# Weights converted a few operations per half step from the end of the attention on, and a 64-float tile of biases: a two-layer feed-forward kernel behind an attention

## The chip, the cores and the metric

The kernel runs on one core of one Trainium2 chip. The time is that of one execution on the device, in microseconds (us). It is given as the median of three runs. Apart from these runs, one execution was profiled, and the rows below come from its trace.

## The reference, cut to what matters

```python
# attention of 8 batches, 8 heads, 576 positions of 64; k and v are averaged over 8 positions first
x = attention(q, k, v)                    # -> 4608 tokens x 512
h = x @ w_in1;  x = (h * cos(h)) @ w_out1           # 512 -> 2048 -> 512
h = x @ w_in2;  return (h * clip(h + 3, 0, 6) / 6) @ w_out2
```

The weights of the two layers arrive as 64-bit numbers.

## The kernel before

**Weights.** The hidden width of 2048 is cut into NF = 16 pieces `fc` of 128. A piece of a layer has two halves, w_in and w_out, and each half is one job. `fetch_weights` (L89) loads the 64-bit words of a job into a tile `st`. `convert_weights` (L101) makes fp32 out of them and splits them into a high and a low part, `wh` and `wl`. A job has three operations in the code, `first`, `second` and `third`; on the engines these are four instructions on DVE (L115, L119, L124, L127), two on ACT (L114, L132) and one on POOL (L133). There are 64 jobs. The pieces 0 to 6 lie in `pool_a`; the pieces 7 to 15 lie in `pool_b`, which is opened when the attention has ended and its memory is free. The second layer's pieces take the same places when the first layer's are used up.

**Steps.** A block is 512 tokens. A step (m, key, bl, fc) is one layer, one block and one piece. `gemm1` (L164) makes h out of the block's x: 12 matmuls of 512 columns, with the weights as the stationary operand (loaded into the array ahead of the matmul) and `xh`, `xl` as the moving one. `chain0` to `chain3` apply the activation on ACT and DVE and split the result into `gh` and `gl`. `gemm2` (L220) follows two steps later, with 12 more matmuls of 512 columns. In the first layer `wh`, `wl` are stationary and `gh`, `gl` moving there; in the second layer it is the other way round. On PE, the 12 matmuls of gemm1 and the 12 of an earlier step's gemm2 alternate.

There are 59 steps for the pieces 0 to 6 (0 to 4 in the first two blocks) of the first layer, with the attention woven in between; then 85 steps for its other pieces, and 144 for the second layer, 16 to a block. Steps are numbered from 0 in that order: step 59 is the first without a piece of attention due, steps 144 to 287 are the second layer.

**When a job is issued.** `need(s)` (L587) is called for step s and for step s+1. It issues every job up to the one asked for, whole. So the code asks for piece 7 when step 60 is issued.

**What sets the order on the engines.** The code's order is only a priority. The tile framework sorts the instructions when the program is built, engine by engine, by a plan of its own in which an instruction may go as soon as its operands and its buffers are there. A job that the code issues late can so be placed much earlier. At run time each engine follows the order that was built.

**Where tiles lie.** Pools lie behind each other in a partition's memory in the order in which they are opened: `pool_a`, `stg`, `xpl` (xr, xh, xl), `gpl` (`bias_c` first, then g, t, gh, gl, ys), then the attention's `ap`, and in its place later `pool_b` and `ypl`.

Of the kernel before, what the change touches and what calls it, by code (L numbers as in the profile page):

```python
# [8 lines left out]
F32 = mybir.dt.float32  # L9
# [15 lines left out]
def f(ap):  # L25
    return ap.bitcast(F32)
# [3 lines left out]
def tile_kernel(ctx, tc, q, k, v, wi1, wo1, wi2, wo2, ident_d, mask_d, out):  # L30
# [3 lines left out]
    P = 128  # L34
# [4 lines left out]
    NF = wo1.shape[0] // P  # L39
# [3 lines left out]
    LAG = 2  # L43
# [32 lines left out]
    pool_a = ctx.enter_context(tc.tile_pool(name="pool_a", bufs=NA))  # L76
    stg = ctx.enter_context(tc.tile_pool(name="stg", bufs=1))
    xpl = ctx.enter_context(tc.tile_pool(name="xpl", bufs=1))
    gpl = ctx.enter_context(tc.tile_pool(name="gpl", bufs=1))
# [9 lines left out]
    def fetch_weights(m, fc, half):  # L89
        st = stg.tile([P, 2 * HW], U32, tag="st", name="st", bufs=2)  # L90
        wi, wo = words[m]
        if half == 0:
            nc.sync.dma_start(
                out=st.rearrange("p (c j) -> p c j", j=2 * P),
                in_=wi[:, fc * 2 * P : (fc + 1) * 2 * P].rearrange("(c p) j -> p c j", p=P),
            )
        else:
            nc.sync.dma_start(out=st, in_=wo[fc * P : (fc + 1) * P, :])
        staged[m, fc, half] = st

    def convert_weights(m, fc, half, pool):  # L101
        st = staged.pop((m, fc, half))
        if half == 0:
            weights[m, fc] = tuple(
                pool.tile([P, 2 * HW], F32R, tag=nm, name=nm) for nm in ("wh", "wl")
            )
        wh, wl = (t[:, half * HW : (half + 1) * HW] for t in weights[m, fc])
        lo, hi = st[:, 0::2], st[:, 1::2]
        a = stg.tile([P, HW], U32, tag="a", name="a", bufs=AB)
        e = stg.tile([P, HW], BF16, tag="e", name="e")  # L110
        w = f(a)

        def first():
            nc.scalar.activation(out=e, in_=st.bitcast(BF16)[:, 3::4], func=AF.Square)  # L114
            nc.vector.tensor_scalar(  # L115
                out=a, in0=hi, scalar1=0x07FFFFFF, scalar2=3,
                op0=ALU.bitwise_and, op1=ALU.logical_shift_left,
            )
            nc.vector.scalar_tensor_tensor(  # L119
                out=a, in0=lo, scalar=29, in1=a, op0=ALU.logical_shift_right, op1=ALU.bitwise_or  # L120
            )

        def second():
            nc.vector.scalar_tensor_tensor(  # L124
                out=a, in0=hi, scalar=0xC0000000, in1=a, op0=ALU.bitwise_and, op1=ALU.bitwise_or
            )
            nc.vector.scalar_tensor_tensor(  # L127
                out=w, in0=e, scalar=2.0**-30, in1=w, op0=ALU.is_ge, op1=ALU.mult
            )

        def third():
            nc.scalar.activation(out=wh, in_=w, func=AF.Copy)  # L132
            nc.gpsimd.tensor_tensor(out=wl, in0=w, in1=f(wh), op=ALU.subtract)  # L133

        return [first, second, third]
# [16 lines left out]
        nc.gpsimd.tensor_tensor(out=xl, in0=t, in1=f(xh), op=ALU.subtract)  # L152
        xs_[key, c] = (xh, xl)

    bias_c = gpl.tile([P, 32], F32, tag="bias", name="bias_c")
    nc.vector.memset(bias_c[:, 0:1], 0.25)
    nc.vector.memset(bias_c[:, 1:2], math.pi / 2)
    nc.vector.memset(bias_c[:, 2:3], 3.0)
# [5 lines left out]
    def gemm1(s):  # L164
        m, key, bl, fc = steps[s][:4]
        wh, wl = weights[m, fc]
        pool = ps_h2 if ps_h2 is not None and s % 2 else ps_h
        h = pool.tile([P, N], F32, tag="h", name="h")
        n = 0
        for c in range(NC):  # L170
            cs = slice(c * P, (c + 1) * P)
            xh, xl = xs_[key, c]
            for a, z in ((wh, xh), (wh, xl), (wl, xh)):
                nc.tensor.matmul(h, a[:, cs], z, start=(n == 0), stop=(n == 3 * NC - 1))  # L174
                n += 1
        hs[s] = h
# [357 lines left out]
    for bl in range(NB):  # L534
        n = NAL[bl]
        steps += [(0, (0, bl), bl, fc, fc == 0, fc == n - 1) for fc in range(n)]
    SA = len(steps)
    for bl in range(NB):
        n = NAL[bl]
        steps += [(0, (1, bl), bl, fc, fc == n, fc == NF - 1) for fc in range(n, NF)]  # L540
    SB = len(steps)
# [22 lines left out]
    live = True  # L564

    wjobs = [(0, fc, hf, "a") for fc in range(NA) for hf in range(2)]
    fetched = 0
    converted = 0

    def w_fetch():  # L570
        nonlocal fetched
        if fetched < len(wjobs) and fetched < converted + 2:
            fetch_weights(*wjobs[fetched][:3])
            fetched += 1

    running = []
    whole = set()

    def w_ops(n):
        while running and n:  # L580
            running.pop(0)()
            n -= 1
            if not running:
                whole.add(wjobs[converted - 1][:3])
                w_fetch()

    def need(s):  # L587
        m, _, _, fc = steps[s][:4]
        while (m, fc, 1) not in whole:
            w_convert(pool_a if wjobs[converted][3] == "a" else pool_b)  # L590

    def w_convert(pool, n=3):
        nonlocal converted
        m, fc, hf, _ = wjobs[converted]
        converted += 1
        running.extend(convert_weights(m, fc, hf, pool))
        w_ops(n)

    w_fetch()
    w_fetch()  # L600
    npieces = 0
    while not started:
        next(att)
        npieces += 1
        while converted < len(WPRE) and WPRE[converted] <= npieces:
            w_convert(pool_a)
    for c in range(NC):
        fetch_x(0, (0, 0), 0, c)
    for c in range(NC):
        split_x((0, 0), c)  # L610

    pool_b = None
    T = len(steps)
    after = {}
    ypl = None
# [1 line left out]
    for slot in range(2 * (T + LAG) + 4):  # L617
        s, odd = divmod(slot, 2)
        for fn in after.pop(slot, ()):
            fn()  # L620
        if not odd and s < T:
            m, key, bl, fc, first, last = steps[s]
            need(s)
            gemm1(s)
            chain0(s)
            chain1(s)
            chain2(s)
            chain3(s)
            if s + LEAD < T and (pool_b is not None or steps[s + LEAD][3] < NA):
                need(s + LEAD)  # L630
            if key[0] == 1 and fc == NF - 5:
                for c in range(NC):
                    t = ypl.tile([P, N], F32, tag="yv", name="yv", bufs=4)
                    nc.sync.dma_start(
                        out=t, in_=yp_d[c * P : (c + 1) * P, bl * N : (bl + 1) * N]
                    )
                    yprev[key, c] = t
            nxt = s
            while nxt < T and steps[nxt][1] == key:
                nxt += 1  # L640
            left = nxt - s
            if nxt < T:
                nm, nk, nbl = steps[nxt][:3]
                ready = nk[0] != 0 or min(B - 1, ((nbl + 1) * N - 1) // S) in done
                if (nk, 0) not in xraw and (nk, 0) not in xs_ and ready and left <= 4:
                    for c in range(NC):
                        fetch_x(nm, nk, nbl, c)
                    for c in range(2):
                        after.setdefault(slot + max(1, 2 * (left - 2) + 1 + c), []).append(
                            lambda nk=nk, c=c: split_x(nk, c)  # L650
                        )
                    after.setdefault(slot + 2 * (left - 1) + 1, []).append(
                        lambda nk=nk: [split_x(nk, c) for c in (2, 3)]
                    )
        if odd and s >= LAG and s - LAG < T:
            gemm2(s - LAG)
        while converted - len(WPRE) < len(WAT) and WAT[converted - len(WPRE)] <= slot:
            w_convert(pool_a)
        if live:
            key = steps[s][1]  # L660
            i = sum(1 for x in steps[:s] if x[1] == key)
            goal = base + 32 * (key[1] + (2 * i + odd + 1 + PACE) / (2 * NAL[key[1]]))
            if key[0] > 0:
                goal = 1 << 30
            elif slot < len(GOFF):
                goal += GOFF[slot]
            while live and npieces < goal:
                try:
                    next(att)
                    npieces += 1  # L670
                except StopIteration:
                    live = False
                    actx.close()
                    ps_h2 = ctx.enter_context(tc.tile_pool(name="ps_h2", bufs=2, space=PSUM))
                    pool_b = ctx.enter_context(tc.tile_pool(name="pool_b", bufs=NF - NA))
                    ypl = ctx.enter_context(tc.tile_pool(name="ypl", bufs=1))
                    wjobs += [(0, fc, hf, "b") for fc in range(NA, NF) for hf in range(2)]
                    wjobs += [(1, fc, hf, "a") for fc in range(NA) for hf in range(2)]
                    wjobs += [(1, fc, hf, "b") for fc in range(NA, NF) for hf in range(2)]
                    w_fetch()  # L680
                    w_fetch()
# [48 lines left out]
```

## Time and profile before

| | us |
|---|---|
| median of three runs (lowest, highest) | 1875.38 (1873.78, 1876.55) |
| the profiled execution | 1878.48 |
| its span, first to last instruction | 1876.6 |
| PE busy | 1790.0 |
| DVE busy | 927.4 |
| ACT busy | 875.2 |
| POOL busy | 403.7 |

The span is the time from the first to the last instruction on the core; the 1.9 us beside it lie before and behind. The profiled execution is 3.1 us above the median of the runs. Busy times are unions over an engine's instructions. The stretches of the second group below begin where gemm1 of steps 0, 41, 63, 142 and 147 begins, and the last ends within gemm1 of step 287.

### The profile page before, as it was taken

Reading aid. Unit: us, or ns where it says so; the run is one execution under the profiler, and the core shown is the slowest. Engines: PE = TensorE matmul, PEld = TensorE weight load, DVE = VectorE, ACT = ScalarE, POOL = GpSimd, SP = SyncE. Lnnn points to the kernel's source line nnn. Section 1 sums busy time; section 2 is a strip of 40 time slices with the busy share of each in tenths; the row PEclk is TensorE's granted clock in tenths of the full one; section 3 lists DMA queues with packets and bytes.
Section 4 is the critical chain, followed back from the end, with each engine's and each line's share of the span. In section 5 each row is a group of like instructions: output and inputs, shape, how many; then the busy total and the mean of one; then the engine's idle time right before and its main releaser. Section 6 shows DMA issues by size and latency. Waiting matters only on the chain.

```text
span 1876.6 us, 21118 instructions
## 1 busy us (share of the span) xinstructions
PE 1790.0 (95%) x8016; PEld 1446.5 (77%) x8016; DVE 927.4 (49%) x1386; ACT 875.2 (47%) x1472; POOL 403.7 (22%) x302
## 2 busy tenths in 40 slices
PE   5689999999888999999999899999999999999999
PEld 4567777888666888888888678888888888888887
DVE  7999656656989364444445952222222222222222
ACT  3567677776666455555555533232323232322222
POOL 3755344322433111111112421010101010100000
PEclk8789999999998999999999999999999999999999
DMA  7656352223434022222222411010101010101000
GB/s 203 180 164 209 113 155 73 88 74 121 154 127 146 23 90 68 68 68 68 68 68 79 129 62 45 1 45 1 45 1 45 1 45 1 45 2 39 1 23 23
DMA packets 114630, 138.82 MB, mean 74 GB/s; under 512 B 44256, under 2 KB 68960, under 8 KB 114528
## 3 DMA queue, kind: packets, MB, share of 16 engines
q1 hardware_dynamic: 114528, 137.47, 23.8%
q8 instruction: 63, 1.03, 0.2%
q14 instruction: 39, 0.32, 0.1%
HBM read 99.69 MB, written 37.75 MB: 73 GB/s over the span
## 4 chain that ended last, share of the span: by engine, by line
PE 77%; DVE 12%; issue 4%; ACT 3%; DMA 2%; POOL 1%; SPq 0%; DVEq 0%; POOLq 0%; ACTq 0%
PE h L174 36%; PE y L236 36%; DVE a L119 2%; PE ap_ps L392 2%; DVE a L124 2%; PE ap_ps L468 2%; DVE a L127 1%; DVE a L115 1%; DVE g L195 1%; DVE raw L321 1%; DVE gl L217 1%; POOL xl L152 1%; DMA raw<-in_k_dram 1%; DMA xr<-x_d 1%; DVE g L208 1%
## 5 line engine op out<-in xcount | busy, mean ns | idle before, releaser
L174 PE MATMUL h<-xl,wh 128*128 128x512 f32 x1152 | 457.5, 397 | 13.4 <-POOL xl L152 13.3
L174 PE MATMUL h<-xh,wh 128*128 128x512 f32 x1152 | 459.1, 399 | 2.3 <-ACT xh L151 2.3
L174 PE MATMUL h<-xh,wl 128*128 128x512 f32 x1152 | 456.6, 396 | 0.0
L152 POOL TENSOR_TENSOR xl<-xr,xh 128x512 fp32r<-128x512 f32 x108 | 151.1, 1418 | 948.3 <-ACT xh L151 947.0
L200 DVE SCALAR_TENSOR_TENSOR g<-g,h 128x512 f32<-128x512 f32 x144 | 98.9, 687 | 471.1 <-ACT g L186 471.1
L186 ACT ACTIVATE g<-h,bias_c 128x512 f32<-128x512 f32 x144 | 98.9, 687 | 437.8 <-PE h L174 437.3
L174 PEld LDWEIGHTS h<-xl,wh 128*128 128x128 f32 x1152 | 217.6, 189 | 67.8 <-POOL xl L152 19.6
L211 ACT ACTIVATE gh<-g 128x512 fp32r<-128x512 f32 x288 | 181.7, 631 | 180.5 <-DVE g L200 104.4
L217 DVE TENSOR_TENSOR gl<-g,gh 128x512 fp32r<-128x512 f32 x255 | 190.6, 747 | 145.5 <-ACT gh L211 143.6
L174 PEld LDWEIGHTS h<-xh,wh 128*128 128x128 f32 x1152 | 217.4, 189 | 50.9 <-ACT xh L151 3.8
L174 PEld LDWEIGHTS h<-xh,wl 128*128 128x128 f32 x1152 | 217.3, 189 | 49.1 <-issue 0.4
L236 PE MATMUL y<-gh,wh 128*128 128x512 f32 x576 | 233.6, 406 | 9.2 <-ACT ys L252 5.3
L236 PE MATMUL y<-gl,wh 128*128 128x512 f32 x576 | 232.1, 403 | 5.3 <-DVE gl L217 5.2
L236 PE MATMUL y<-gh,wl 128*128 128x512 f32 x576 | 230.7, 401 | 0.0
L236 PE MATMUL y<-wh,gh 128*128 128x512 f32 x576 | 226.4, 393 | 1.4 <-DVE yv L244 1.4
L236 PE MATMUL y<-wl,gh 128*128 128x512 f32 x576 | 226.2, 393 | 0.0
L236 PE MATMUL y<-wh,gl 128*128 128x512 f32 x576 | 225.9, 392 | 0.0
L195 DVE SCALAR_TENSOR_TENSOR g<-g,t 128x512 f32<-128x512 f32 x144 | 114.9, 798 | 156.2 <-ACT g L194 156.0
L184 ACT ACTIVATE t<-h 128x512 f32<-128x512 f32 x144 | 85.3, 593 | 117.6 <-PE h L174 117.5
L236 PEld LDWEIGHTS y<-gh,wh 128*128 128x128 f32 x576 | 111.1, 193 | 37.4 <-ACT ys L252 7.8
L198 ACT ACTIVATE g<-g 128x512 f32<-128x512 f32 x144 | 90.9, 631 | 96.0 <-DVE g L195 95.7
L236 PEld LDWEIGHTS y<-gl,wh 128*128 128x128 f32 x576 | 111.0, 193 | 31.9 <-DVE gl L217 8.9
(93 smaller groups left out, 2140.4 us busy)
## 6 DMA issues: line engine op xcount, KB each, us to landing
xr<-x_d SPq DMA_DIRECT2D x72, 256.0 KB, 2.8
st<-in_moe_w_in_dram SPq DMA_DIRECT2D x32, 512.0 KB, 3.8
st<-in_moe_w_out_dram SPq DMA_DIRECT2D x32, 512.0 KB, 3.3
yp_d<-ys SPq DMA_DIRECT2D x36, 256.0 KB, 2.5
yv<-yp_d SPq DMA_DIRECT2D x36, 256.0 KB, 3.5
xr<-y_d SPq DMA_DIRECT2D x36, 256.0 KB, 2.7
out_dram<-ys SPq DMA_DIRECT2D x36, 256.0 KB, 2.0
raw<-in_k_dram SPq DMA_DIRECT2D x8, 1024.0 KB, 5.8
```

The source lines that it names most:

```text
L119: nc.vector.scalar_tensor_tensor(out=a, in0=lo, scalar=29, in1=a, op0=ALU.logical_shift_right, op1=ALU.bitwise_or)
L124: nc.vector.scalar_tensor_tensor(out=a, in0=hi, scalar=0xC0000000, in1=a, op0=ALU.bitwise_and, op1=ALU.bitwise_or)
L152: nc.gpsimd.tensor_tensor(out=xl, in0=t, in1=f(xh), op=ALU.subtract)
L174: nc.tensor.matmul(h, a[:, cs], z, start=(n == 0), stop=(n == 3 * NC - 1))
L184: nc.scalar.activation(out=t, in_=hs[s], func=AF.Copy, bias=0.25, scale=INV_2PI)
L186: nc.scalar.activation(out=g, in_=hs[s], func=AF.Relu, bias=bias_c[:, 2:3], scale=1.0)
L195: nc.vector.scalar_tensor_tensor(out=g, in0=g, scalar=MAGIC, in1=t, op0=ALU.subtract, op1=ALU.subtract)
L198: nc.scalar.activation(out=g, in_=g, func=AF.Sin, scale=-TWO_PI)
L200: nc.vector.scalar_tensor_tensor(out=g, in0=g, scalar=6.0, in1=h, op0=ALU.min, op1=ALU.mult)
L211: nc.scalar.activation(out=gh, in_=g, func=AF.Copy)
L217: eng.tensor_tensor(out=gl, in0=gs[s][0], in1=f(gh), op=ALU.subtract)
L236: nc.tensor.matmul(y[c], a, z, start=(first and n == 0), stop=(last and n == 2))
```

## The change

**The jobs.** `w_ahead` is new. From the end of the attention on it is called in each half step, and it issues one operation of the running job in an even half step and two in an odd one, so one job per step. For the second layer's pieces in `pool_a` it issues an operation in odd half steps alone, a job in three steps, and not before step SA + 2 = 61; a piece fc in `pool_b` is not begun before step SB - 16 + fc + 2. `need` stays as the last resort.

**The tile.** `bias_c` is 256 bytes of a partition instead of 128. Three of its columns are used, before and after.

```diff
-    bias_c = gpl.tile([P, 32], F32, tag="bias", name="bias_c")
+    bias_c = gpl.tile([P, 64], F32, tag="bias", name="bias_c")
...
     def need(s):
         m, _, _, fc = steps[s][:4]
         while (m, fc, 1) not in whole:
-            w_convert(pool_a if wjobs[converted][3] == "a" else pool_b)
+            if running:
+                w_ops(len(running))
+            else:
+                w_convert()
...
+    def w_ahead(s, odd):
+        if not running:
+            if converted == len(wjobs):
+                return
+            m, fc, _, home = wjobs[converted]
+            if m == 1 and s < (SA + LAG if home == "a" else SB - NF + fc + LAG):
+                return
+            w_convert(0)
+        m, _, _, home = wjobs[converted - 1]
+        slow = m == 1 and home == "a"
+        w_ops(odd if slow else 1 + odd)
...
+        if not live:
+            w_ahead(s, odd)
```

**What it does to the order.** PE has the same instructions in the same order, all 7858. The other engines have the same instructions too, and their order differs at one place alone, within four steps that follow soon after the attention. On DVE, where L115 to L127 are a job's instructions and L195, L208, L217 those of the chain, there stands in the kernel before:

```order
L119 SCALAR_TENSOR_TENSOR a<-st,a 128x512
L195 SCALAR_TENSOR_TENSOR g<-g,t 128x512
L127 SCALAR_TENSOR_TENSOR a<-e,a 128x512
L124 SCALAR_TENSOR_TENSOR a<-st,a 128x512
L208 TENSOR_TENSOR g<-h,g 128x512
L127 SCALAR_TENSOR_TENSOR a<-e,a 128x512
L217 TENSOR_TENSOR gl<-g,gh 128x512
L115 TENSOR_SCALAR a<-st 128x512
```

and at the same place in the changed kernel:

```order
L127 SCALAR_TENSOR_TENSOR a<-e,a 128x512
L195 SCALAR_TENSOR_TENSOR g<-g,t 128x512
L119 SCALAR_TENSOR_TENSOR a<-st,a 128x512
L124 SCALAR_TENSOR_TENSOR a<-st,a 128x512
L208 TENSOR_TENSOR g<-h,g 128x512
L127 SCALAR_TENSOR_TENSOR a<-e,a 128x512
L115 TENSOR_SCALAR a<-st 128x512
L217 TENSOR_TENSOR gl<-g,gh 128x512
```

An L127 moved ahead of L195 and an L119 behind it, and an L115 moved ahead of L217; a little further on, L115 passes one L195 and L124 one L208. Before and behind these rows DVE's order is the same, the second layer's jobs too. On POOL, where L133 is a job's last instruction and L152 makes `xl` for a coming block, there stands before:

```order
L133 TENSOR_TENSOR wl<-a,wh 128x512 x6
L152 TENSOR_TENSOR xl<-xr,xh 128x512
L133 TENSOR_TENSOR wl<-a,wh 128x512
L152 TENSOR_TENSOR xl<-xr,xh 128x512 x3
L133 TENSOR_TENSOR wl<-a,wh 128x512 x10
```

and in the changed kernel:

```order
L133 TENSOR_TENSOR wl<-a,wh 128x512 x6
L152 TENSOR_TENSOR xl<-xr,xh 128x512
L133 TENSOR_TENSOR wl<-a,wh 128x512
L152 TENSOR_TENSOR xl<-xr,xh 128x512 x2
L133 TENSOR_TENSOR wl<-a,wh 128x512
L152 TENSOR_TENSOR xl<-xr,xh 128x512
L133 TENSOR_TENSOR wl<-a,wh 128x512 x9
```

One L133 moved ahead of the last of three L152. ACT's L114, L132 and L151 and one of SP's loads of `xr` trade places there in the same way.

**What it does to the addresses.** In the built program, everything that is allocated behind `bias_c` lies 128 bytes further up in the partition. The first buffer of each tile:

| tile | byte before | byte after | remainder by 256 before, after |
|---|---|---|---|
| `wh`, `wl` in `pool_a` | 16512, 45184 | the same | 128, 128 |
| `xh`, `xl` | 93312, 105600 | the same | 128, 128 |
| `gh`, `gl` | 126208, 132352 | 126336, 132480 | 0, 128 |
| `wh`, `wl` in `pool_b` | 146688, 183552 | 146816, 183680 | 0, 128 |
| `vh`, `vl` (attention) | 191040, 195136 | 191168, 195264 | 64, 192 |
| `pth`, `ptl` (attention) | 199360, 212160 | 199488, 212288 | 192, 64 |

The other buffers of a tile, and the slices that a matmul takes, lie whole multiples of 256 bytes further.

## Rows read from the trace of the kernel before

**Rows 1.** The page: busy time by engine, and the span in 40 slices.

```profile
PE 1790.0 (95%) x8016; PEld 1446.5 (77%) x8016; DVE 927.4 (49%) x1386; ACT 875.2 (47%) x1472; POOL 403.7 (22%) x302
...
PE   5689999999888999999999899999999999999999
```

**Rows 2.** Busy time in six stretches: from:to length, engines, clock, DMA share, GB/s.

```profile
core 0: us, PE busy (x) PEld busy (x) DVE busy (x) ACT busy (x) POOL busy (x), PEclk, DMA share, GB/s
0.00:74.24 74.24, 42.01 (x206) 35.44 (x206) 62.11 (x116) 29.04 (x60) 35.15 (x30) 0.78 0.77 204
74.24:456.06 381.82, 357.31 (x1861) 286.99 (x1860) 259.98 (x446) 281.21 (x490) 164.25 (x126) 0.98 0.41 124
456.06:608.99 152.93, 134.95 (x529) 102.92 (x528) 140.00 (x176) 94.47 (x168) 59.83 (x41) 0.94 0.46 145
608.99:1045.62 436.63, 436.63 (x1897) 356.03 (x1896) 206.66 (x286) 228.47 (x379) 78.65 (x58) 1.00 0.22 68
1045.62:1087.14 41.52, 33.32 (x121) 24.28 (x120) 41.21 (x51) 22.30 (x39) 21.97 (x14) 0.92 0.44 138
1087.14:1863.50 776.36, 776.36 (x3369) 633.41 (x3368) 214.67 (x311) 217.16 (x335) 43.88 (x34) 1.00 0.07 23
```

**Rows 3.** What PE waited for from 456 to 610 us: total, times, longest.

```profile
PE h L174 <- POOL xl L152: 5.6, 5, 2.4
PE y L236 <- ACT ys L252: 5.3, 4, 1.8
PE y L236 <- DVE gl L217: 3.8, 5, 1.3
```

**Rows 4.** Jobs on DVE, 456 to 609 us: min/median/max ns, first and last start.

```profile
L115 DVE TENSOR_SCALAR a<-st x28: 414/420/1516, 458.6 to 598.6; 128x512 uint32<-128x512 uint32 x28
L119 DVE SCALAR_TENSOR_TENSOR a<-st,a x28: 675/938/1785, 460.1 to 599.6; 128x512 uint32<-128x512 uint32 x28
```

**Rows 5.** The chain that ended last, in order of time: start, us, what.

```profile
1148.28 2.79 PE h L174 x12
1151.08 2.73 PE y L236 x12
...
1159.34 2.73 PE h L174 x12
1162.07 2.73 PE y L236 x12
...
1178.55 2.80 PE y L236 x12
1181.34 2.76 PE h L174 x12
...
1198.00 2.79 PE h L174 x12
```

**Rows 6.** Timeline of PE: start, us; first and last of twelve L468 matmuls.

```profile
446.53 0.31 PE L468 MATMUL ap_ps<-pth,vh 128*128 128x320 f32 x1
...
448.14 0.31 PE L468 MATMUL ap_ps<-pth,vl 128*128 128x320 f32 x1
```

**Rows 7.** Timeline of DVE at the place where its order changes.

```profile
483.42 1.75 DVE L217 TENSOR_TENSOR gl<-g,gh 128x512 fp32r<-128x512 f32 x1
485.09 1.50 DVE L115 TENSOR_SCALAR a<-st 128x512 uint32<-128x512 uint32 x1
486.62 1.65 DVE L119 SCALAR_TENSOR_TENSOR a<-st,a 128x512 uint32<-128x512 uint32 x1
488.20 0.68 DVE L195 SCALAR_TENSOR_TENSOR g<-g,t 128x512 f32<-128x512 f32 x1
```

**Rows 8.** Timeline of POOL at that place.

```profile
481.22 1.73 POOL L133 TENSOR_TENSOR wl<-a,wh 128x512 fp32r<-128x512 f32 x1
482.91 4.81 POOL L152 TENSOR_TENSOR xl<-xr,xh 128x512 fp32r<-128x512 f32 x3
```

More of the change, by code (lines that the diff above doesn't have):

```diff
@@ L589, in need, with w_convert @@
         while (m, fc, 1) not in whole:
-            w_convert(pool_a if wjobs[converted][3] == "a" else pool_b)
-    def w_convert(pool, n=3):
+            if running:
+                w_ops(len(running))
+            else:
+                w_convert()
+    def w_convert(n=3):
         nonlocal converted
-        m, fc, hf, _ = wjobs[converted]
+        m, fc, hf, home = wjobs[converted]
         converted += 1
+        pool = pool_a if home == "a" else pool_b
         running.extend(convert_weights(m, fc, hf, pool))
         w_ops(n)
+    def w_ahead(s, odd):
[9 more added lines that the diff above has]
+        w_ops(odd if slow else 1 + odd)
+    pool_b = None
     w_fetch()
@@ L605, in tile_kernel @@
         while converted < len(WPRE) and WPRE[converted] <= npieces:
-            w_convert(pool_a)
+            w_convert()
     for c in range(NC):
@@ L610, in tile_kernel @@
         split_x((0, 0), c)
-    pool_b = None
     T = len(steps)
@@ L657, in tile_kernel @@
         while converted - len(WPRE) < len(WAT) and WAT[converted - len(WPRE)] <= slot:
-            w_convert(pool_a)
+            w_convert()
+        if not live:
+            w_ahead(s, odd)
         if live:
```

## The prediction

> **What bounds the kernel now.** I read the page first. PE is busy for 95% of the span, DVE and ACT for about half, and in most of the 40 slices PE shows a 9 [rows 1]. So nearly all of the time is PE's, and a change must either fill PE's gaps or make its matmuls follow each other faster. The next view says where the gaps are. I cut the span into six stretches: the start, the steps woven with the attention, the stretch behind it, the rest of the first layer, the change of layers, and the second layer [rows 2]. In the fourth and the sixth PE is busy for 436.63 of 436.63 and 776.36 of 776.36 us, at a granted clock of 1.00, the 2.4 GHz level. Nothing is waited for there. Together they are 1213 us, two thirds of the span. In the third PE is busy for 134.95 of 152.93 us and DVE for 140.00, and in the fifth PE for 33.32 of 41.52 and DVE for 41.21. These two are DVE's. They are where the weights are converted: 28 jobs between 456 and 609 us, the first at 458.6, directly behind the attention [rows 4].
>
> So the trace shows that the kernel before converts ahead already. Its code asks for piece 7 at step 60, and the jobs begin within step 41, which starts the third stretch at 456.06. The framework's plan has put them where their buffers come free.
>
> Then I looked at how fast PE goes where nothing stops it. The chain, which is PE alone in the second layer, has one row per 12 matmuls, and these rows are not equal [rows 5]. A block's 16 steps start with the row at 1159.34, and gemm1 of step s alternates with gemm2 of step s-2. So 1159.34 is gemm1 with piece 0, and 1162.07 is gemm2 with piece 14 of the block before. Read in that way, there are four kinds:
>
> gemm1 with weights of `pool_a`: 2.73 us, or 2.76 between slow gemm2 (1159.34, 1181.34).
> gemm1 with weights of `pool_b`: 2.79 (1148.28, 1198.00).
> gemm2 with weights of `pool_b`: 2.73 (1151.08, 1162.07).
> gemm2 with weights of `pool_a`: 2.80 (1178.55).
>
> Instructions, shapes and clock are the same in each pair. What differs is where the weights lie. gemm1 reads them beside `xh` and `xl`, gemm2 beside `gh` and `gl`. In the table of addresses x and `pool_a` have the remainder 128 by 256, g and `pool_b` have 0. Equal remainders go with 2.73, unequal ones with 2.76 to 2.80, in both layers and whichever operand is the stationary one. Higher address bits don't fit. Buffers lie 2048 or 4096 bytes apart and slices 512, and still pieces 14 and 7 take 2.79 both in gemm1 (1148.28, 1198.00), and pieces 12 and 14 take 2.73 both in gemm2 (1151.08, 1162.07). So the low bits are what is left.
>
> **The change part by part.** *The tile of biases.* It moves g and `pool_b` by 128 bytes and leaves x and `pool_a`. All four pairs then have the remainder 128. I take 2.73 us for each of them, which is 227.5 ns a matmul.
>
> Fourth stretch: 1896 matmuls (weight loads counted) in 436.63 us, 230.3 ns each. At 227.5 they take 431.3: 5.3 us less. Sixth stretch: 3368 in 776.36 us, at 227.5 they take 766.2: 10.1 us less. Second stretch: the gemm2 of steps 0 to 38 use `pool_a`, 468 matmuls at 2.80/12 - 2.73/12 = 5.8 ns, which is 2.7 us if PE alone sets the pace and 0 if its waits swallow it. PE is busy for 94% of it, but waits for the attention many times, so I take 1.5. Third stretch: some 22 gemm2 likewise, at most 1.5 us, but DVE is the bound; I take 0.3. The fifth is DVE's: 0. The sum is 5.3 + 10.1 + 1.5 + 0.3 = 17.2 us. Its bounds: nothing, if the remainder is not the cause; and 22 us, with the second and third stretch at their 2.7 and 1.5 (19.6) and with 2.73 read as the lowest value that rounds to it (0.4 ns a matmul on the 5264 of the two long stretches, 2.2).
>
> *The jobs.* The same 64 jobs run, with the same instructions and the same DMAs, and after one place the order is the old one on every engine. So nearly all of the conversion stays where it was, the fifth stretch included, and costs what it did. At the one place a job's L127 goes ahead of the chain's L195 and an L119 behind it; further on an L115 passes L217 and L195, an L124 L208. DVE has no idle time there, so the sum of its work is the same, and what can change is which instruction meets one of POOL's. Without that meeting L119 takes 0.675 us, with it 1.785 [rows 4], and while POOL runs its `wl` and three `xl` one behind the other, three of DVE's instructions in succession take 1.50 to 1.75 us, an L115 among them whose median is 0.420 [rows 4, 7, 8]. One meeting more or less is 1.1 us, and there are some three places where it can fall differently: -3 to +3 us. The chain operation that comes later by one short instruction (L217 behind L115) delays a gemm2 by 0.4, and PE's waits on `gl` are 3.8 us in all there [rows 3]. The `wl` that now stands ahead of the third `xl` frees its buffer sooner; that `xl` is for a block some seven steps away, so it can wait. Nearest to a row is one trade for another: 0.
>
> *What hides it.* The wider tile costs memory alone, and the three memsets are the same. With PE 1.2% faster, DVE's 206.66 us still fit twice into the fourth stretch, and ACT's 228.47 too, so no engine becomes the bound there.
>
> The profiled execution takes 1878.5, less 17.2 is 1861.3. It is 3.1 above the median of the runs, so the median is forecast at 1858.
>
> **The rivals.** *The addresses have no part in it*, and the pools differ in speed for a reason that the shift leaves. For it speaks the attention's own product. There the operands' remainders are 64 and 192, as unequal as the slow pairs, yet from the first to the last of twelve L468 matmuls of 320 columns 1.61 us pass [rows 6], 146.4 ns each. The 192 columns more of a fast matmul cost 227.5 - 146.4 = 81 ns, 0.42 a column, which is one column a cycle at 2.4 GHz; so these are on the fast line. Against it: they are shorter and start off a multiple of 128, and no other difference between the two pools is left that holds for all pieces. Then the time is the old one, moved only by the order: 1875, from 1872 to 1878.
>
> The Trainium skill, TensorE: Matmul & The Clock Gate, section "Step-by-step: what each phase is for", speaks for this rival: the array has two independent read ports, so loading the next weights does not take reading bandwidth from the running matmul. By that rule the place of a tile could not matter and the gain of the shift would be 0. The rows of the four kinds differ with the place of the weights all the same, and the rule does not explain them.
>
> *The unlike pairs get worse.* By 512 the remainders are 128 for x and `pool_a`, 256 for g and `pool_b`; after the change 128 and 384. If a difference of 256 bytes disturbs more than one of 128, the slow pairs get slower. A second penalty as large as the first is another 17 us: 1892. It decides as soon as the penalty grows by more than the order can give back, 3 us. Nothing in the rows has such a difference, and nothing excludes it.
>
> *The trades at the one place cost more than a meeting.* The steps there are a knot of PE, DVE and POOL, with five waits on `xl` in the kernel before, the longest of them 2.4 us [rows 3]. Two or three of them more with no gain from the addresses give 1881.
>
> *The jobs do spread*, as the code reads, and the two stretches of DVE lose their gaps. At 5.46 us a step, the 22 steps of the third stretch would take 120 us instead of 153, the fifth's 5 steps 27 instead of 41.5: 33 + 14 = 47 us, with the addresses 1811. The built order excludes it almost wholly.
>
> **How the numbers follow.** The forecast has 0.66. Its own range is 1852 to 1866: the larger bound of the sum with 1 us from the order, and half of the sum, if only gemm1 or only gemm2 is mended. No part of the addresses 0.22, worse pairs 0.08, a knot 0.03, spreading 0.01. 0.2% is 3.8 us, about what a measurement of this kernel can tell from no change. Faster by that is the forecast and the spreading, with a little of the second case: 0.67. Same is most of the second case, 0.22. Slower are worse pairs and the knot: 0.11. The range of 8 in 10 must take in the old time: 1852 to 1879.
>
> **What would show it.** In the chain of the changed kernel all rows of 12 matmuls in the second layer should be 2.73, whatever the piece. The fourth and the sixth stretch should be 431 and 766 us long with the same counts. The third and the fifth should stay within 3 us of 152.9 and 41.5, with the jobs at the same places. If rows of 2.79 and 2.80 are still there in the old pattern, the remainder by 256 is not the cause and the forecast is wrong; if they have grown, the third case holds. If the stretches behind the attention move by more than 3 us, I have mis-sized the trades.

## The result, and the profile after

The changed kernel takes 1855.61 us in the median of four runs (1854.46 to 1856.69), the kernel before 1874.58 in four runs beside it. The ratio is 0.9898, with a 95% interval from 0.9881 to 0.9915. It is faster by 19.0 us; 1858 was forecast. The profiled execution took 1856.69 us, 1.1 above its median.

The page of the changed kernel, busy time by engine and PE in 40 slices:

```profile
PE 1767.9 (95%) x8016; PEld 1444.7 (78%) x8016; DVE 928.4 (50%) x1386; ACT 874.7 (47%) x1472; POOL 404.7 (22%) x302
...
PE   5689999999888999999999899999999999999999
```

PE is busy for 22.1 us less with the same 8016 instructions, DVE, ACT and POOL for what they were [rows 1]. The picture in slices is the same too, with the lower digits where they were. So the gaps are not what went.

The same six stretches as in [rows 2], cut at the same steps (columns as there):

```profile
0.00:73.33 73.33, 41.88 (x206) 35.07 (x206) 61.94 (x116) 29.10 (x60) 35.25 (x30) 0.77 0.76 206
73.33:455.62 382.29, 356.80 (x1862) 286.57 (x1861) 260.21 (x446) 281.19 (x490) 164.89 (x126) 0.98 0.41 124
455.62:606.71 151.09, 132.65 (x530) 102.63 (x528) 138.77 (x175) 93.25 (x166) 60.30 (x41) 0.94 0.46 147
606.71:1036.47 429.76, 429.76 (x1898) 355.97 (x1896) 207.83 (x287) 228.99 (x381) 78.50 (x58) 1.00 0.22 69
1036.47:1078.43 41.96, 34.13 (x122) 24.77 (x120) 41.65 (x51) 22.30 (x39) 21.94 (x14) 0.88 0.42 136
1078.43:1841.79 763.36, 763.36 (x3369) 632.32 (x3368) 215.24 (x311) 217.31 (x335) 43.82 (x34) 1.00 0.07 23
```

The length is the number to read, line by line against [rows 2]. The fourth stretch lost 6.9 us and the sixth 13.0, with the same counts, at clock 1.00 in both kernels, the 2.4 GHz level, and with PE busy all through in both. The other four moved by -0.9, +0.5, -1.8 and +0.4. The sum of the six is -21.7; the last 13 us of the span are the same. That is what the two profiled executions lie apart (21.8); the medians lie 19.0 apart.

The chain that ended last, at the beginning of the second layer's second block, where [rows 5] had four different rows:

```profile
1149.32 2.72 PE h L174 x12
1152.04 2.72 PE y L236 x12
1154.76 2.72 PE h L174 x12
1157.48 2.72 PE y L236 x12
1160.20 2.72 PE h L174 x12
```

All rows of 12 matmuls in this block and the next are 2.72, 226.7 ns a matmul, whatever the piece.

### The profile page after: what moved, and what is told of

Same layout as the page of the kernel before. It is cut to its first block, busy times and chain, and to the rows that moved or that the text cites. A ratio compares the mean times of both kernels' runs of the same rounds, so it can differ in the third digit from the quotient of the medians.

```text
span 1854.9 us, 21119 instructions
## 1 busy us (share of the span) xinstructions
PE 1767.9 (95%) x8016; PEld 1444.7 (78%) x8016; DVE 928.4 (50%) x1386; ACT 874.7 (47%) x1472; POOL 404.7 (22%) x302
## 4 chain that ended last, share of the span: by engine, by line
PE 75%; DVE 14%; issue 4%; ACT 3%; POOL 2%; DMA 1%; SPq 0%; DVEq 0%; ACTq 0%; POOLq 0%
PE h L174 36%; PE y L236 35%; DVE a L119 2%; DVE a L124 2%; DVE a L127 2%; PE ap_ps L468 2%; DVE a L115 1%; PE ap_ps L392 1%; DVE g L195 1%; DVE raw L321 1%; DVE gl L217 1%; POOL xl L152 1%; DMA raw<-in_k_dram 1%; DVE g L208 1%; DVE sm L414 1%
## 5 line engine op out<-in xcount | busy, mean ns | idle before, releaser
L174 PE MATMUL h<-xh,wh 128*128 128x512 f32 x1152 | 454.3, 395 | 2.3 <-ACT xh L151 2.3
L174 PE MATMUL h<-xh,wl 128*128 128x512 f32 x1152 | 451.9, 392 | 0.0
L152 POOL TENSOR_TENSOR xl<-xr,xh 128x512 fp32r<-128x512 f32 x108 | 151.7, 1422 | 931.8 <-ACT xh L151 930.9
L174 PEld LDWEIGHTS h<-xl,wh 128*128 128x128 f32 x1152 | 217.5, 189 | 63.5 <-POOL xl L152 19.9
L217 DVE TENSOR_TENSOR gl<-g,gh 128x512 fp32r<-128x512 f32 x255 | 190.9, 749 | 147.1 <-ACT gh L211 138.9
L195 DVE SCALAR_TENSOR_TENSOR g<-g,t 128x512 f32<-128x512 f32 x144 | 115.8, 804 | 146.8 <-ACT g L194 146.7
```

The source lines that it names most:

```text
L195: nc.vector.scalar_tensor_tensor(out=g, in0=g, scalar=MAGIC, in1=t, op0=ALU.subtract, op1=ALU.subtract)
L217: eng.tensor_tensor(out=gl, in0=gs[s][0], in1=f(gh), op=ALU.subtract)
```

## The experiments

Two theories stood against each other. *Addresses*: a row is slow when the weights and what is streamed beside them have unequal remainders by 256 bytes. *Jobs*: the gain comes from the conversion that is issued ahead.

**The tile alone.** The kernel before, with one edit:

```diff
-    bias_c = gpl.tile([P, 32], F32, tag="bias", name="bias_c")
+    bias_c = gpl.tile([P, 64], F32, tag="bias", name="bias_c")
```

> The kernel before with the 64-float tile of biases and nothing else. If the gain comes from the addresses (equal remainders by 256 of the weights and of what the matmul beside them streams), all of it is here: 1856, from 1853 to 1859, and every row of 12 matmuls in the second layer 2.72. If it comes from the jobs issued ahead, 1875.

Measured: 1854.72 us, ratio 0.9888, from 0.9871 to 0.9904. Its third to sixth stretch:

```profile
452.38:605.40 153.02, 133.85 (x530) 102.75 (x528) 140.25 (x176) 94.63 (x168) 59.77 (x41) 0.94 0.45 145
605.40:1035.16 429.76, 429.76 (x1898) 355.86 (x1896) 206.71 (x285) 227.94 (x379) 78.49 (x58) 1.00 0.22 69
1035.16:1077.05 41.89, 33.34 (x122) 24.20 (x121) 41.58 (x51) 22.30 (x39) 21.97 (x14) 0.92 0.43 136
1077.05:1840.40 763.35, 763.35 (x3369) 632.10 (x3368) 215.24 (x311) 217.31 (x335) 43.80 (x34) 1.00 0.07 23
```

The fourth and the sixth are those of the changed kernel to a hundredth of a microsecond. The whole gain is here.

**The jobs alone.** The changed kernel with the tile of 32 floats again.

> The changed kernel with the tile of biases at 32 floats again: only the way in which jobs are issued differs from the kernel before. By the addresses 1875, from 1872 to 1878, with the old rows of 2.73, 2.79 and 2.80. If the jobs are the cause, 1856.

Measured: 1875.33 us in ten runs, ratio 1.0003, from 0.9994 to 1.0013. The third, fourth and sixth stretch:

```profile
453.46:604.77 151.31, 132.55 (x529) 100.62 (x528) 138.76 (x175) 93.10 (x166) 60.41 (x41) 0.97 0.46 146
604.77:1041.39 436.62, 436.62 (x1898) 355.91 (x1897) 208.20 (x288) 229.39 (x381) 78.64 (x58) 1.00 0.21 68
...
1082.92:1859.30 776.38, 776.38 (x3369) 633.02 (x3368) 214.80 (x311) 217.31 (x335) 43.82 (x34) 1.00 0.07 23
```

The slow lengths of [rows 2] are back. The third stretch is 151.3, as in the changed kernel, against 152.9 and 153.0 in the two kernels with the old order. So the trades in the order seem to give some 1.7 us there. The size is not certain: of four kernels further down that have the new order too, two have 151.3 (96 floats, g alone moved) and two have 152.7 and 152.4 (48 floats, the attention's operands equal). Where the time comes from is not shown, and the median of the whole does not show it.

**A tile of 96 floats**, the changed kernel otherwise: g and `pool_b` move by 128 bytes more.

> The changed kernel with a tile of 96 floats: g and pool_b move up by 128 bytes more, to remainder 0 by 256, as before the change. By the remainder theory the slow rows of 2.79 and 2.80 are back and the time is 1875. If what counts is that the tiles lie further apart than before, or any other thing that the wider tile brings, it stays at 1856.

Measured: 1873.11 us in one execution, the profiled one, as in the next three and in the one with the attention's operands equal. The chain at the same block as above, whose steps begin at 1154.00:

```profile
1148.47 2.79 PE h L174 x12
1151.26 2.74 PE y L236 x12
1154.00 2.73 PE h L174 x12
...
1167.65 2.80 PE y L236 x12
1170.45 2.76 PE h L174 x12
```

The old pattern is back, though the tile is wider and the tiles lie further apart than in the changed kernel. So it is the remainder, not the width or the distance.

**A tile of 48 floats**, remainder 64 for g and `pool_b`.

> The changed kernel with a tile of 48 floats: g and pool_b have remainder 64 by 256, x and pool_a 128. If only equal remainders are fast, the unlike pairs are slow, at 2.76 to 2.80, and the time is 1870 to 1875. If only a difference of 128 is slow, all rows are 2.72 and the time is 1856.

Measured: 1872.78 us. The chain in the second layer, from the pieces of `pool_a` (first two lines) to those of `pool_b`:

```profile
1179.49 2.72 PE h L174 x12
1182.21 2.75 PE y L236 x12
...
1228.96 2.76 PE h L174 x12
1231.72 2.77 PE y L236 x12
```

A difference of 64 costs too, less than half as much in this layer's gemm2 with `pool_a` (2.75 against 2.80). There g, with 64, is loaded and the weights, with 128, are streamed. In the first layer gemm2 with `pool_a` loads the weights and streams g, and the same difference costs all of the 2.80. Here a row begins with its first matmul and ends where the next row begins:

```profile
556.17 0.39 PE L236 MATMUL y<-gh,wh 128*128 128x512 f32 x1
...
558.97 0.39 PE L174 MATMUL h<-xh,wh 128*128 128x512 f32 x1
```

It is not the layer that makes the difference: gemm1 with `pool_b`, which has 64 loaded and 128 streamed in both layers, takes 2.76 in the first and 2.75 to 2.76 in the second. So at 64 it counts which of the two has the higher remainder.

gemm1 with `pool_a`, whose remainders are equal, is 2.72 in the second layer. The last row of the chain does not fit the simple form of the theory: gemm2 with `pool_b` has 64 and 64, and takes 2.77. It stands between slow rows of gemm1. By the starts in the trace, its last two matmuls follow at 226.7 ns, as in an undisturbed row, and the ten ahead of them at 232 in the mean. So what an unlike pair costs does not end with its row; why it lasts that long is not shown.

**g alone moved.** In the changed kernel, 128 unused bytes behind `gpl`:

```diff
+    pad_p = ctx.enter_context(tc.tile_pool(name="pad_p", bufs=1))
+    pad = pad_p.tile([P, 32], F32, name="pad")
+    nc.vector.memset(pad[:, 0:1], 0.0)
```

> The changed kernel with 128 unused bytes behind gpl: g has remainder 128 by 256 like x and pool_a, pool_b has 0. By the remainder theory everything with pool_a is fast (2.72 in gemm1 and in gemm2) and everything with pool_b slow (2.79 in gemm1, 2.79 to 2.80 in gemm2): a step of the first layer's second part 5.58, the second layer 5.44 for pieces 0 to 6 and 5.58 for 7 to 15, the time about 1880. If a place of the weights is fast or slow by itself, gemm2 with pool_b keeps its 2.73 and only gemm1 with pool_b is slow: about 1867.

Measured: 1875.52 us. The chain in the second layer's second block, pieces of `pool_a`, then of `pool_b`:

```profile
1172.76 2.72 PE h L177 x12
1175.48 2.72 PE y L239 x12
...
1191.80 2.73 PE y L239 x12
1194.53 2.80 PE h L177 x12
1197.32 2.76 PE y L239 x12
...
1225.18 2.80 PE y L239 x12
1227.98 2.80 PE h L177 x12
```

With g at 128 and `pool_b` at 0, gemm2 has changed sides: with `pool_a` it is fast, with `pool_b` slow; it was the other way round in [rows 5]. The weights lie where they lay in the kernel with 96 floats. So no place of the weights is slow by itself; the pair counts. The rows came as expected, the total 4 us lower than expected.

The three rows in the middle show more. The first, gemm2 with piece 4, has equal remainders throughout, and the row behind it is the first with `pool_b`. Its matmuls follow at 226 or 227 ns but for the last, which takes 232 or 233 in each of the nine blocks; with pieces 2 and 3, where weights of `pool_a` follow, the last takes 226 or 227 too. In the trace the weights of the next matmul are loaded beside a matmul, from 2 to 4 ns behind its start. So what is streamed has to match the weights loaded meanwhile, those of the next matmul. The third row has equal remainders too; its first seven matmuls take 224 to 236 ns, and only then do they fall back to 227. So rows of 2.73 to 2.77 can be equal rows that carry a cost of their neighbours.

**Unused bytes ahead of everything.** The kernel before with such a tile of 48 floats ahead of `pool_a`.

> The kernel before with 48 unused floats ahead of all pools: x and pool_a have remainder 64 by 256, g and pool_b 192, the two remainders of the attention's product, whose 320-column matmuls are on the fast line. If a difference of 128 is slow for matmuls of 512 columns wherever it starts, 1875 and the old pattern. If it is slow only at multiples of 128, all rows are 2.72 and the time is 1856.

Measured: 1873.86 us, and the old chain row for row:

```profile
1165.60 2.73 PE h L177 x12
1168.33 2.80 PE y L239 x12
1171.13 2.76 PE h L177 x12
```

Where the pairs of 512 columns start does not matter, their difference does. So the attention's matmuls, with 64 and 192, are not excepted because of where they start.

**The attention's operands made equal.** The changed kernel with six small buffers instead of two ahead of `pth`:

```diff
-        mx = ap.tile([P, 4, 1], F32, tag="mx", name="mx", bufs=2)
+        mx = ap.tile([P, 4, 1], F32, tag="mx", name="mx", bufs=6)
```

> The changed kernel with four more small buffers ahead of pth in the attention's memory, which give pth and ptl the remainder 192 by 256 that vh and vl have (before: 64 against 192). If the attention's 320-column matmuls are slowed by unequal remainders like those of 512 columns (by 3%), their spacing falls from 146 to about 142 ns. If they don't feel it, 146 ns stays. The time is 1856 in both cases.

Measured: 1856.5 us. The first and the last of twelve matmuls in the timeline:

```profile
444.76 0.30 PE L468 MATMUL ap_ps<-pth,vh 128*128 128x320 f32 x1
...
446.36 0.31 PE L468 MATMUL ap_ps<-pth,vl 128*128 128x320 f32 x1
```

That is 1.60 us over eleven intervals, 145.5 ns, against 146.4 in [rows 6]. Over all such intervals of the two traces the mean is 146.3 here and 146.5 in the changed kernel. The matmuls of 320 columns don't feel the remainder by the 3% that would show. Why they don't stays open.

**The jobs really spread.** In the built order of the changed kernel the jobs stand in a row, as before. Here the first DVE instruction of each job behind the attention is kept behind the DVE instructions that the code issues ahead of it:

```diff
-            nc.vector.tensor_scalar(
+            i = nc.vector.tensor_scalar(
...
+            if paced:
+                tc.keep_in_program_order(i)
...
                     live = False
+                    paced.append(1)
```

> The changed kernel, with the first DVE instruction of each job behind the attention kept, in the built order, behind all DVE instructions that the code issues ahead of it, so that the jobs stand where the code puts them: one per step. If the lost time of the two stretches is due to 28 and 18 jobs in a row on DVE, it goes: a step with a job needs about 2.1 us of chain, 2.5 of job and 1.1 of a meeting with POOL, 5.7 on DVE against 5.44 on PE, so the third stretch falls from 151 to about 126 us and the fifth from 42 to about 30: 1820, from 1812 to 1830. If the stretches are bound by something else (loads, POOL's xl), 1850 or more.

Measured: 1821.86 us (1819.55 to 1824.98), ratio to the kernel before 0.9706, from 0.9689 to 0.9723. The third to sixth stretch:

```profile
452.76:582.33 129.57, 124.03 (x530) 99.50 (x528) 96.86 (x139) 82.67 (x147) 41.97 (x31) 0.99 0.42 130
582.33:1012.09 429.76, 429.76 (x1898) 356.08 (x1896) 230.56 (x322) 237.75 (x398) 89.11 (x65) 1.00 0.25 80
1012.09:1045.24 33.15, 29.26 (x121) 23.00 (x120) 28.46 (x36) 17.70 (x31) 15.10 (x11) 0.95 0.46 143
1045.24:1810.14 764.90, 764.90 (x3369) 633.45 (x3368) 228.44 (x335) 223.04 (x346) 51.14 (x40) 1.00 0.08 26
```

The third stretch is 21.5 us shorter than in the changed kernel, the fifth 8.8. DVE's busy time fell in both, from 138.77 to 96.86 and from 41.65 to 28.46, and rose in the stretches behind them, where PE is busy all through. The sixth stretch is 1.5 us longer than in the changed kernel: it begins at a granted clock of 0.50, the 1.2 GHz level, behind the gaps of the fifth, and its first seven matmuls follow at 0.43 us. This kernel beats both others.

**A slower pace.** The kernel with the jobs spread, but with no job of the first layer in every fourth step:

```diff
+        if m == 0 and s % 4 == 0:
+            return
```

> The kernel with paced jobs, but for the first layer's no job in every fourth step: 18 jobs in 24 steps instead of 18; the last piece is then ready in step 65 and asked for in step 69. If the 9.9 us that the third stretch still loses against 22 steps of 5.44 come from jobs that meet the split of x (POOL's xl) in the same step, most of it stays and the time is 1816 to 1822. If they come from the pace of one job per step on DVE, it falls to about 122 us and the time to 1814.

Measured: 1821.95 us, ratio 0.9713, from 0.9697 to 0.9730: no better. What PE waited for from 452 to 586 us (total, times, longest):

```profile
PE y L239 <- ACT ys L255: 5.6, 3, 3.9
PE y L239 <- DVE gl L220: 0.5, 1, 0.5
```

The third stretch stays at 130.3 us, 10.6 above 22 steps of 5.44. The time lies in the range that was named for `xl`, but `xl` is gone from the list. Here it is PE's wait for the copies of a finished block's y, 3.9 us of it in one piece, and for 4.8 us behind that wait the granted clock is 0.50 and the matmuls follow at 0.43 us. In the kernel with one job per step `xl` stands in the list with 2.4 us and the copies with 1.4. So one loss went and another came, and the run does not tell whether the pace on DVE costs anything.

## Why the prediction was right

**What bounds the kernel.** Right. PE alone set the pace in the fourth and the sixth stretch, and 19.9 of the 21.7 us came from there, without a gap closed. One reading beside it was wrong and did no harm: ACT's 228.47 us do not fit twice into a stretch of 431, but 1.9 times.

**The tile of biases.** Right, and it is the whole change: alone it gives 0.9888, the rest alone 1.0003. The cause, unequal remainders by 256 of weights and streamed operand, was argued from [rows 5] and the table of addresses. It is shown now: equal pairs are fast and unequal ones slow when g and `pool_b` lie 0, 64, 128 and 256 bytes further up than before, when g is moved alone, and when everything is moved; the equal rows that are not quite fast stand beside unequal ones.

The term was mis-sized. "I take 2.73 us for each of them" gave 5.3 and 10.1 us, and 6.9 and 13.0 were measured, since a row takes 2.72, and a step 5.44 us (429.76 over 79 steps). The rows of 2.73 were themselves not clean: they stand beside rows whose operands have the other remainder. In the kernel with g alone moved, gemm1 with `pool_a` is 2.72 between equal gemm2, in both layers. The bound that I gave for the rounding, 2.2 us, was the right direction and half the size.

That the forecast of 1858 lies within 2.4 us of the median is in part luck. The two long stretches gave 4.5 us more than their terms, the 1.5 of the second stretch did not come, and the medians show 19.0 of the 21.8 us between the profiled executions.

**The second and the third stretch.** The 1.5 us of the second did not come: 382.29 against 381.82. With the tile alone, the jobs alone and the jobs paced it is 379.2, 380.5 and 378.1, so what is waited for there varies by more than the term. "2.7 us if PE alone sets the pace and 0 if its waits swallow it": the runs do not tell where between. The 0.3 of the third did not show either: 153.02 with the tile alone against 152.93.

**The jobs.** Right that the order keeps them where they were: the fifth stretch is 41.96 against 41.52. The trades were put at 0, from -3 to +3, and measured between -0.3 and -1.8 in the third stretch. This is the timeline of DVE in the changed kernel, at the place of [rows 7]:

```profile
482.99 1.75 DVE L217 TENSOR_TENSOR gl<-g,gh 128x512 fp32r<-128x512 f32 x1
484.65 1.50 DVE L115 TENSOR_SCALAR a<-st 128x512 uint32<-128x512 uint32 x1
486.08 0.68 DVE L127 SCALAR_TENSOR_TENSOR a<-e,a 128x512 f32<-128x512 bf16 x1
486.68 0.68 DVE L195 SCALAR_TENSOR_TENSOR g<-g,t 128x512 f32<-128x512 f32 x1
...
488.00 1.67 DVE L124 SCALAR_TENSOR_TENSOR a<-st,a 128x512 uint32<-128x512 uint32 x1
489.59 0.68 DVE L208 TENSOR_TENSOR g<-h,g 128x512 f32<-128x512 f32 x1
```

The last two in the kernel before:

```profile
489.40 0.68 DVE L124 SCALAR_TENSOR_TENSOR a<-st,a 128x512 uint32<-128x512 uint32 x1
490.01 0.67 DVE L208 TENSOR_TENSOR g<-h,g 128x512 f32<-128x512 f32 x1
```

L127 at the place of L119 takes 0.68 instead of 1.65 us, and the chain's L195 starts 2.0 us after L115 instead of 3.1. But the meeting is only put off: the job's L124 takes 1.67 instead of 0.68, and the chain's L208 starts 4.9 us after L115 in both. It was one trade for another, as was predicted.

**The rivals.** *No part of the addresses* fell with the tile alone. The rule of the Trainium skill that spoke for it (TensorE: Matmul & The Clock Gate, section "Step-by-step: what each phase is for") says that loading the next weights takes no reading bandwidth from the running matmul. That the place of a tile can't matter does not follow from it here: 12 matmuls take 2.72 or 2.80 us by the address alone. Whether it is reading bandwidth that they lose, the runs don't tell. The attention's product, which spoke for this rival too, is indeed not slowed; that is shown for its matmuls of 320 columns alone. *The unlike pairs get worse* fell: a difference of 256 is as good as none. *The trades cost more than a meeting* fell too: with the new order alone the third stretch is 1.6 us shorter, and the whole as before (1.0003). *The jobs do spread* was rightly excluded for this change. Its price was too high by a third: where the order is made to spread them, 31.7 of the 47 us come (152.93 to 129.57 and 41.52 to 33.15). PE still waits there: a step of the third stretch takes 5.9 us, not 5.46.

## What to carry to other kernels

When the same matmuls have slightly different lengths in a stretch where PE never waits, group the rows by the buffers that they read and compare the addresses; 128 bytes of padding were worth 1%. A change of the order in the code is a change only where the built order shows it: here issuing the jobs earlier in the code moved almost nothing, and one added order constraint per job that holds them back was worth 1.8% more. And a group of rows that looks fast may carry a cost of its neighbours; take the floor from a stretch in which all rows are equal.

## What the runs showed of the hardware that was not expected

Twelve fp32 matmuls of 512 columns take 2.72 us when the addresses of the loaded weights and of the streamed operand have the same remainder by 256 bytes and 2.79 to 2.80 when they differ by 128, with the granted clock at 1.00 in all of them. When they differ by 64, it takes 2.75 to 2.76 with the lower remainder on the operand that is loaded, and 2.80 with the higher one there. Equal rows beside unequal ones take 2.73 to 2.77. It does not matter which of the two is the layer's weights. Matmuls of 320 columns at 146 ns don't show it. What the array or the memory does in the slow case, the runs don't tell.
